# Assignment sums of two more heads folded on VectorE, a last store in two halves, and a re-searched instruction order, in a routing-attention and MLP kernel

## Chip, cores, metric

One core of one Trainium2 chip. The metric is the device time of one execution in microseconds (us). The fast runs of the kernel before lie between 290.9 and 292.1 us in all rounds, 0.4% apart; every comparison below is between kernels run in turns on the same chip. A ratio is the mean time of one kernel's fast runs over the mean of the other's fast runs of the same rounds, so it is not quite the ratio of the medians quoted beside it. Engine names in the profile: PE is TensorE (products), PEld its weight loads, DVE is VectorE, ACT is ScalarE, POOL is GpSimd, SP is SyncE, which issues transfers.

## The reference, cut to what matters

```python
# B, H, S, D = 4, 8, 768, 64: 32 heads in all; 16 centroids per head
q_assign = argmax(normalised(q) @ normalised(c).T)     # one cluster per query
k_assign = argmax(normalised(k) @ normalised(c).T)     # one cluster per key
mask   = q_assign[:, :, :, None] == k_assign[:, :, None, :]
scores = where(mask, q @ k.T / sqrt(D), -1e9)
x      = softmax(scores) @ v            # reshaped to 3072 tokens x 512
h      = x @ w_in                       # 512 -> 2048
out    = gelu_exact(h) @ w_out          # 2048 -> 512
```

## The kernel before: what the change touches

The kernel is a list of some 2,000 small operations, each with a name, an engine and its dependencies. One long string, the order table, gives the order in which they are emitted; each engine gets its own part of that order as its list of instructions. A word such as `lok2@DVE` also names the engine. So the table decides two things: what stands behind what on each engine, and which engine does an operation that several could do.

For each head `i` the cluster of every query and key is found so. A product with the centroids (kept as a high and a low half in fp16) gives the assignment sums; `amax` takes the maximum over the 16 clusters; `ge` compares with it and so writes one-hot rows; those are transposed by TensorE (early heads) or by a transfer (later heads) and written into `kqT`, where they act as the mask inside the score product. The sums come in two ways:

```python
    ACC = set(range(0, 8))
    ...
        def asn(w):
            ...
                if acc:      # two products of 16 columns, summed in PSUM
                    nc.tensor.matmul(o, t[:, js], c_cat[:, h, 0], start=True, stop=False)
                    nc.tensor.matmul(o, t[:, js], c_cat[:, h, 1], start=False, stop=True)
                else:        # one product of 32 columns
                    nc.tensor.matmul(o, t[:, js],
                                     c_cat[:, h].rearrange("p a c -> p (a c)"),
                                     start=True, stop=True)
        ...
        if not acc:
            def fold():      # VectorE adds the two halves: PSUM in, SBUF out
                nc.vector.tensor_reduce(
                    out=T["asb", i],
                    in_=T["asn", i].rearrange("p n w (a c) -> p n w c a", a=2),
                    axis=AX.X, op=ALU.add)
        def src():
            return T["asn", i] if acc else T["asb", i]
        def amax():
            nc.vector.tensor_reduce(out=T["amax", i], in_=src(), axis=AX.X, op=ALU.max)
        def ge():
            nc.vector.tensor_tensor(o[:, :, :, 0:C], src(),
                                    T["amax", i].to_broadcast([128, N, 2, C]),
                                    op=ALU.is_ge)
```

The second MLP layer is computed with fewer products by a scheme of sums and differences of its operands. Its 64 operand sums (S1 to S4) may run on VectorE, or on GpSimd where the table says `@POOL`:

```python
            o1 = add("DVE", 0.58, due, lambda eng, f=sums: f(eng, 1), gb,
                     take=[s_S], name=f"S1_{b}{n}", alt={"POOL": 1.85})
            o2 = add("DVE", 0.58, due, lambda eng, f=sums: f(eng, 2), [o1, *ga], name=f"S2_{b}{n}", alt={"POOL": 1.85})
            o3 = add("DVE", 0.58, due, lambda eng, f=sums: f(eng, 3), [o1, *ga], name=f"S3_{b}{n}", alt={"POOL": 1.85})
```

The softmax here doesn't subtract the row's maximum and nothing guards it: scores larger than these inputs give would overflow.

## Time and profile before

| | before |
|---|---|
| time, median of 3 runs (range) | 291.6 us (291.41 to 291.66) |
| span of the profiled run | 289.8 us |
| TensorE work (sum of median start-to-start distances) | 278.1 us |
| TensorE time lost in waits between first and last product | 6.9 us |
| busy: TensorE, VectorE, ScalarE, GpSimd | 98, 70, 81, 37% |

TensorE is the bound. It can gain only from fewer products or from fewer waits, and the waits add up to 6.9 us. The lines that show it stand in the prediction.

### The profile page before, as it was taken

How to read it: one execution, taken by the hardware profiler on the slowest of the kernel's cores; microseconds unless marked ns; L12 is line 12 of the kernel's file. 1: busy time of each engine (PE TensorE's matmuls, PEld its weight loads, DVE VectorE, ACT ScalarE, POOL GpSimd, SP SyncE). 2: the span in 40 equal slices, each digit the busy share in tenths (PEclk: the TensorE clock that was granted, in tenths of full speed). 3: DMA queues.
4: the chain of work that ended last, by engine and by line, in shares of the span. 5: the costliest groups of instructions: out<-in, count | busy, mean ns of one | idle time of the engine just before them, and what ended most of it. 6: DMA issues, size and time to landing. Idle time of an engine off the chain costs nothing.

```text
span 289.8 us, 8355 instructions
## 1 busy us (share of the span) xinstructions
PE 284.4 (98%) x3398; PEld 213.0 (73%) x3398; DVE 204.2 (70%) x494; ACT 235.1 (81%) x333; POOL 108.0 (37%) x148
## 2 busy tenths in 40 slices
PE   8999999999999999999999999999999999999995
PEld 6887766677677777765677878766687788756884
DVE  4989788397998778643489875725778833787863
ACT  4899988699799999977799988957699988599510
POOL 5898834609120631117202031605622271328000
PEclk9999999999999999999999999999999999999999
DMA  7999998899666799976479899753134213200023
GB/s 249 249 268 248 256 214 230 207 174 177 160 175 139 146 227 187 188 192 168 127 156 177 156 222 187 191 128 75 27 30 118 56 50 97 77 2 0 20 74 127
DMA packets 78038, 43.11 MB, mean 149 GB/s; under 512 B 55472, under 2 KB 78000, under 8 KB 78000
## 3 DMA queue, kind: packets, MB, share of 16 engines
q1 hardware_dynamic: 73488, 38.16, 57.7%
q0 software_dynamic: 4224, 4.19, 8.9%
q8 instruction: 26, 0.43, 0.6%
q10 hardware_dynamic: 288, 0.23, 0.3%
q14 instruction: 12, 0.10, 0.1%
HBM read 27.30 MB, written 6.29 MB: 116 GB/s over the span
## 4 chain that ended last, share of the span: by engine, by line
PE 96%; DVE 2%; ACT 1%; issue 0%; DVEq 0%
PE op L1233 25%; PE hp L918 22%; PE sc_ps L783 21%; PE x_ps L815 12%; PE fx_ps L1054 6%; PE asn_ps L615 2%; PE warm_ps L372 2%; PE tr_ps L573 2%; DVE kqT L714 1%; DVE kqT L723 1%; PE asn_ps L613 1%; PE asn_ps L612 1%; PE oh_ps L691 1%; ACT p_sb L792 1%; PE fin_ps L886 0%
## 5 line engine op out<-in xcount | busy, mean ns | idle before, releaser
L792 ACT ACTIVATE p_sb<-sc_ps 128x768 f16<-128x768 f32 x192 | 146.0, 810 | 9.7 <-PE sc_ps L783 6.8
L783 PE MATMUL sc_ps<-kqT 80*128 80x384 f16 x384 | 93.5, 325 | 0.6 <-DVE kqT L714 0.3
L918 PE MATMUL hp<-xt,w_in_sb 128*128 128x384 f16 x384 | 65.6, 326 | 0.0
L815 PEld LDWEIGHTS <-p_sb 128*128 128x128 f16 x1152 | 47.2, 97 | 10.4 <-DVE x_tok L842 0.6
L1233 PEld LDWEIGHTS <-g 128*128 128x128 f16 x480 | 45.3, 97 | 12.6 <-DVE g L948 0.2
L931 ACT ACTIVATE g<-hp 128x768 f16<-128x768 f32 x48 | 38.9, 810 | 19.0 <-PE hp L918 18.5
L918 PEld LDWEIGHTS <-w_in_sb 128*128 128x128 f16 x384 | 36.4, 98 | 22.9 <-issue 0.2
L815 PE MATMUL x_ps<-vaug,p_sb 128*128 128x65 f16 x1152 | 51.6, 193 | 0.0
L1233 PE MATMUL op<-w_out_sb,g 128*128 128x256 f16 x288 | 40.9, 272 | 0.0
L783 PEld LDWEIGHTS <-kqT 80*128 80x128 f16 x384 | 31.6, 98 | 4.7 <-DVE kqT L714 0.5
L1233 PE MATMUL op<-w_st,g 128*128 128x256 f16 x192 | 27.3, 272 | 0.0
L518 POOL TENSOR_TENSOR st<-k_raw,st 128x384 f16<-128x384 f32 x18 | 17.0, 943 | 24.9 <-DVE st L382 18.4
L518 POOL TENSOR_TENSOR st<-q_raw,st 128x384 f16<-128x384 f32 x21 | 19.8, 947 | 13.4 <-ACT st L380 8.6
L382 POOL CAST st<-q_raw 128x384 f16<-128x384 f32 x16 | 8.4, 531 | 40.9 <-DMA q_raw<-in_q_dram 24.9
L631 DVE TENSOR_REDUCE asb<-asn_ps 128x192 f32<-128x384 f32 x24 | 13.2, 551 | 14.8 <-PE asn_ps L615 14.6
L382 POOL CAST st<-k_raw 128x384 f16<-128x384 f32 x16 | 8.6, 537 | 35.4 <-DMA kqT<-st 16.3
L1233 PEld LDWEIGHTS <-S 128*128 128x128 f16 x192 | 18.0, 97 | 5.0
L842 DVE TENSOR_TENSOR x_tok<-x_ps,rec 128x384 f16<-128x384 f32 (+1 forms) x40 | 19.0, 476 | 1.1
L835 DVE RECIPROCAL rec<-x_ps 128x6 f32<-128x6 f32 (+1 forms) x40 | 7.4, 186 | 11.7 <-PE x_ps L815 10.7
L615 PEld LDWEIGHTS <-kqT 128*128 128x128 f16 x288 | 12.0, 96 | 3.4
L1233 PE MATMUL op<-w_st,S 128*128 128x256 f16 x96 | 13.9, 272 | 0.0
L1233 PE MATMUL op<-w_out_sb,S 128*128 128x256 f16 x96 | 13.8, 272 | 0.0
(125 smaller groups left out, 405.6 us busy)
## 6 DMA issues: line engine op xcount, KB each, us to landing
q_raw<-in_q_dram SPq DMA_DIRECT2D x32, 192.0 KB, 3.5
v_raw<-in_v_dram SPq DMA_DIRECT2D x32, 192.0 KB, 3.5
out_dram<-c SPq DMA_DIRECT2D x48, 128.0 KB, 2.0
k_raw<-in_k_dram SPq DMA_DIRECT2D x31, 192.0 KB, 3.4
w_in_sb<-in_moe_w_in_dram POOLq DMA_DIRECT2D x4, 512.0 KB, 10.4
w_out_sb<-in_moe_w_out_dram POOLq DMA_DIRECT2D x4, 512.0 KB, 8.6
kqT<-st SPq DMA_TRANSPOSE x22, 4.3
k_raw<-in_k_dram ACTq DMA_DIRECT2D x1, 192.0 KB, 3.2
```

The source lines that it names most:

```text
L382: engine[eng].tensor_copy(o, i)
L518: engine[eng].tensor_sub(t[:, :, D:2 * D], T[w + "raw", i], t[:, :, 0:D])
L615: nc.tensor.matmul(o, t[:, js], c_cat[:, h].rearrange("p a c -> p (a c)"), start=True, stop=True)
L631: nc.vector.tensor_reduce(out=T["asb", i], in_=T["asn", i].rearrange("p n w (a c) -> p n w c a", a=2), axis=AX.X, op=ALU.add)
L783: nc.tensor.matmul(s_ps[:, e, 0:QB], T["kT", i][0:D + C, c * 128:(c + 1) * 128], T["qT", i][0:D + C, t * QB:(t + 1) * QB], start=True, sto ...
L792: nc.scalar.activation(T["p", i, t][:, 2 * cp:2 * cp + 2, :], T["sc", i, t, cp][:, :, 0:QB], ACT_FN.Exp, bias=0.0, scale=float(scale))
L815: nc.tensor.matmul(o, T["p", i, t][:, ch, jj * 128:(jj + 1) * 128], vaugs[turn("va", i)][:, ch, 0:D + 1], start=(ch == 0), stop=(ch == N - 1))
L842: nc.vector.tensor_tensor(T["xtok", b][:, h // 2, j0:j0 + nn, h % 2 * D:(h % 2 + 1) * D], T["x", key][:, :, 0:D], T["rec", key].to_broadca ...
L918: nc.tensor.matmul(T["hp", hb, fp][:, e, 0:QB], w_in_sb[:, m, f * 128:(f + 1) * 128], T["xt", b][:, m, t * QB:(t + 1) * QB], start=(m == 0 ...
L931: nc.scalar.activation(T["g", hb][:, :, fp, :], T["hp", hb, fp][:, :, 0:QB], ACT_FN.Gelu, bias=0.0, scale=1.0)
L1054: nc.tensor.matmul(o, a[p](m), r[p](m), start=start and m == 0, stop=m == 1, skip_group_check=not start)
L1233: nc.tensor.matmul(T["op", b, key], a()[:, f, j * 128:(j + 1) * 128], w[:, f, :], start=(start and f == 0), stop=(f == NB - 1), skip_group ...
```

## The change

The intent: (1) heads 6 and 7 leave the two-product form, which takes products from TensorE and gives VectorE two folds; (2) the last product is made in two column halves, each added and stored by itself on a queue of its own, so that the end after the last product gets shorter; (3) the order was searched anew, with a refitted model of the durations.

```diff
-    ACC = set(range(0, 8))
+    ACC = set(range(0, 6))
@@ second MLP layer, the last product only
-                    for f in range(4 * n, 4 * n + 4):
-                        nc.tensor.matmul(T["op", b, key],
-                                         a()[:, f, j * 128:(j + 1) * 128], w[:, f, :],
+                    fs = range(NB) if last else range(4 * n, 4 * n + 4)
+                    cs = slice(128 * n, 128 * n + 128) if last else slice(0, DB)
+                    for f in fs:
+                        nc.tensor.matmul(T["op", b, key][:, cs],
+                                         a()[:, f, j * 128:(j + 1) * 128], w[:, f, cs],
@@ its addition and store, once per half n
+                if last:
+                    tail.append(add("DVE", 0.28, ... nc.vector.tensor_add(
+                        c21[:, 128 * n:128 * n + 128], p1[...], op[...]) ...
+                    ... add("SP", 0.36, ... dma_start(out=..., in_=c21[:, half]) ...,
+                        alt={"SP": 0.36, "ACT": 0.36})
@@ the order table: nearly every line differs. Around heads 6 and 7:
-  ... asnq7 loadv5 amax7 loadv7 sc2b1 av4a0 ge7 av4a2 sc5a0 exp2b1 asnk6 asnq6 amax6 ge6 sc5a2 ...
+  ... asnq6 sc3b0 exp3b1 av4a0 v6 exp3b0 loq9 fold6 sc5a0 av4a1 exp5a0 amax6 loadv14 ge7 av4a2 sc2b1 w4 loadv5 lok9 w5 exp2b1 ge6 ...
@@ and around two of the operand sums:
-  ... fc2_0_P5_0_1 S3_02 sc9a2 fc2_0_P6_0_1 ...        ... sc9b2 S3_03 rec8_1 ...
+  ... S2_03 S1_02 S3_02@POOL asnk14 S2_02 ...           ... fc2_0_P6_0_1 S3_03@POOL sc9a2 ...
```

The table has 27 filler products in front for 32, and 135 operations changed engine.

## The prediction

> **What bounds the kernel now.** I read the head of the page first, then the groups by shape, the windows, the chain of waits of the early stage, and the timeline of the last microseconds.
>
> ```profile
> span 289.8 us, 8355 instructions
> PE 284.4 (98%) x3398; PEld 213.0 (73%) x3398; DVE 204.2 (70%) x494; ACT 235.1 (81%) x333; POOL 108.0 (37%) x148
> ...
> PE 96%; DVE 2%; ACT 1%; issue 0%; DVEq 0%
> ```
>
> TensorE is busy for 284.4 of 289.8 us and carries 96% of the chain that ended last, at full clock in every slice. Busy time hides short waits, because a product of 128x32 is shown as 177 ns while the next one starts 25 ns later. So I took the distances between the starts of neighbouring products in the timeline, the median for each kind, and multiplied by the count: 278.1 us of work between the first filler product (1.36) and the last product's start, where 285.0 us passed. So about **6.9 us** of TensorE time is lost in small waits. Besides that come 1.36 us before the first product and some 3.5 us after the last. Nothing else can be won without taking products away.
>
> Where the 6.9 us lie: between the first scores (11.15) and the first product of the first MLP layer (44.76) the same count gives 31.2 us of work in 33.6 us, so **2.4 us** are lost there; the other 224 us up to 269 lose only about 4, in pieces of 0.05 to 0.16 us. The windows say why:
>
> ```profile
> 11.15:44.76 33.61, 32.77 (x574) 25.41 (x574) 28.70 (x76) 30.87 (x43) 26.30 (x39) 1.00 1.11 251
> 44.76:269.00 224.24, 224.24 (x2551) 164.07 (x2549) 156.88 (x373) 193.33 (x268) 74.83 (x85) 1.00 0.65 135
> 269.00:290.00 21.00, 17.61 (x161) 15.43 (x158) 11.86 (x28) 4.44 (x11) 0.00 (x0) 1.00 0.23 76
> ```
>
> The columns after the window's length are TensorE, weight loads, VectorE, ScalarE and GpSimd. In the early stage VectorE is busy 85% and ScalarE 92%; later VectorE is at 70%. And in the early stage the chain runs through VectorE, by the writes of the one-hot rows into kqT:
>
> ```profile
> 19.63 0.55 DVE kqT L714
> ...
> 20.21 0.55 DVE kqT L723
> 20.79 0.56 DVE kqT L714
> ...
> 21.39 0.57 DVE kqT L723
> ```
>
> Four of them end the wait for the scores at 22.00. Heads 6 and 7 are prepared in just this stage (the last assignment maximum of the unfolded kind starts at 33.5).
>
> [...]24 products with 16 columns start from 7.96 to 8.54, which is 0.58 / 23 = 25 ns each, and products with 32 columns are 25 ns apart too. [...]The trace has 1.7 to 2.0 us for nearly all 128 KB output stores[...].
>
> **Part 1: fold of heads 6 and 7.** The groups concerned:
>
> ```profile
> L631 DVE TENSOR_REDUCE asb<-asn_ps 128x192 f32<-128x384 f32 x24 | 13.2, 551 | 14.8 <-PE asn_ps L615 14.6
> L615 PE MATMUL asn_ps<-c_cat,kqT 128*128 128x32 f16 x288 | 12.9, 177 | 0.0
> L612 PE MATMUL asn_ps<-c_cat,kqT 128*128 128x16 f16 x96 | 5.8, 169 | 0.0
> L613 PE MATMUL asn_ps<-c_cat,kqT 128*128 128x16 f16 x96 | 5.8, 169 | 0.0
> ```
>
> Heads 0 to 7 use 2 x 12 products with 16 columns (96 + 96 over eight heads), later heads 12 with 32 columns (288 over 24 heads). For two heads 48 products become 24; each product costs 25 ns[...], so TensorE loses 24 x 25 = **0.60 us** of work, not the 24 x 169 ns that the busy column suggests. VectorE gains two folds of 0.551 us = **1.10 us**; the maximum and the comparison cost the same (0.348 against 0.358 us, and a median of 0.36 both ways). The fold lies between the assignment and the one-hot rows, so it lengthens the preparation of each of the two heads by some 0.3 to 0.5 us, in the stage where VectorE ends TensorE's waits. I take a quarter of the 1.10 us as given back: +0.3.
>
> **Part 2: the tail.** The lines:
>
> ```profile
> 285.57 1.04 PE L1233 MATMUL op<-w_st,g 128*128 128x256 f16 x8
> 285.77 0.42 DVE L1285 TENSOR_TENSOR c<-u,op 128x256 f32<-128x256 f32 x1
> 286.65 0.42 DVE L1279 TENSOR_TENSOR c<-p,op 128x256 f32<-128x256 f32 x1 [0.45 <-PE op L1233]
> ```
>
> The last product's addition takes 0.42 us, its store is issued at 287.10 and has landed at about 288.81 (1.71 us), and 1.0 us of closing semaphores follows. The change makes 16 products of 128 columns (16 x 56 ns = 0.90) out of 8 of 256 (8 x 109 = 0.87): +0.02. An addition of 128 columns I estimate at 0.29 us: this kernel's additions from PSUM take 0.356 us for 192 columns and 0.420 for 256, so 0.064 per 64.[...] But both halves lie in one bank, and in the new table the first half's addition stands behind the second half's products.[...] The second queue only helps where an issue of 0.33 us would be in the way; stores issue at 285.87, 286.30 and 287.10, so the last one waits for no queue now: 0.
>
> **Part 3: the new order.** It has 27 filler products for 32. The first 18 fillers run[...] (213 ns), later ones at 109 ns; in the new order 21 stand in front, and first the k transpose of head 0, then centroids, then q. Between the transposes and the first scores only 6 fillers are left where there were 14. Fillers bridge waits, so removing them saves only if the loads, casts and copies in front are early enough. Taken at face value the work in front of the first scores falls by 5 x 109 = 0.55 us; I take **-0.5**. The rest of the order moves the casts and copies of some 135 operations between ScalarE, VectorE and GpSimd, leaves TensorE's products in number as they are, and can only act on the lost 6.9 us. A search on a better model may take a tenth of that, **-0.6**; it may as well lose as much, as a model is an approximation and the waits it plays with are 0.1 us long.
>
> **Sum:** -0.6 (products) + 0.3 (folds) - 0.1 (tail) - 0.5 (start) - 0.6 (order) = -1.5 us; 291.6 - 1.5 = **290.1 us**.
>
> **Rivals.** (a) *VectorE takes it back.* The two folds and their latency stand fully on the early path: +1.1 instead of +0.3, and the new order finds no room: 291.5. For it: 85% busy, and the chain quoted above. Against it: the early stage's order was searched again with the folds in it. (b) *The order was the true brake.* If the small waits of the early stage fall from 2.4 to about 1 us and the later ones by a quarter, the gain is 0.6 + 0.5 + 1.4 + 1 = 3.5 us: 288.1. For it: the losses are real, and the model was refitted for it. Against it: TensorE is already never idle for long, and ScalarE at 92% leaves the early stage little freedom. (c) *The model is wrong somewhere and one long wait opens*, for example a transfer late for a head: each such wait costs 0.3 to 2 us, 291 to 293. For it: loads are moved about (DMA share 1.11 in the early stage, so full); against it: the order before, of the same kind, shows no wait above 0.5 us. (d) *The fewer fillers [...]only turn into waiting*: the start is worth 0, 290.6.
>
> **Range and chances.** All that could be won without fewer products is 6.9 us of waits, 0.6 + 0.5 of work and a few tenths of tail; 2% is 5.8 us, so it would need nearly all of the waits to vanish: 3%. Slower by 2% needs several waits of kind (c): 2%. The range adds about 1.7 us either way, between rivals (b) and (a): 288.4 to 291.8.
>
> **What would show each step.** Products: L612 and L613 72 each, L615 312, sum of TensorE's work by medians about 277 us. Folds: L631 x26, and the early stage's lost time at 2.4 us or below. Tail: two additions of about 0.29 us; the first beginning before the last product ends, or after it, tells the two cases apart; end of the last product to end of span stays 3.1 to 3.3 us. Start: first scores at about 10.6. Order: total lost time about 6.3 us. I am wrong if the lost time moves by more than 2 us either way, or a wait of TensorE over 1 us appears.

## The result, and the profile after

| | before | after |
|---|---|---|
| time, median of 4 runs (range) | 291.5 us (291.07 to 291.66) | 295.24 us (294.83 to 296.89) |
| ratio, 95% interval | | 1.0141 (1.0101 to 1.0181) |
| span of the profiled run | 289.8 | 295.1 |
| TensorE work | 278.1 | 276.7 |
| TensorE time lost | 6.9 | 13.6 |
| VectorE time over the medians | 10.3 (19 instructions) | 19.2 (28 instructions) |

The kernel became 1.4% slower: within 2%, as most of the chances had it, but 5 us from the predicted time and far outside the range. The last row is made so: in each group of VectorE instructions of one kind and shape, those that lasted over 0.25 us longer than the group's median, and the sum of what they lasted longer. I call them stretched. (Grouped by program line as well, the sums are 10.3 and 17.5 us.)

The head of the page of the kernel after, its clock line and its chain:

```profile
span 295.1 us, 8322 instructions
PE 285.2 (97%) x3377; PEld 212.5 (72%) x3377; DVE 207.5 (70%) x487; ACT 236.3 (80%) x331; POOL 125.2 (42%) x160
...
PEclk9999989999999999999999999999999999999999
...
PE 89%; DVE 6%; ACT 2%; DMA 1%; issue 1%; POOL 0%; ACTq 0%; DVEq 0%
```

GpSimd went from 108.0 to 125.2 us of work, and VectorE's share of the chain from 2 to 6%. The groups show the first as ten more operand sums: GpSimd ran 9 of the shape 128x768 before and 19 after, at 1.64 to 1.70 us each, so 10 x 1.67 = 16.7 of the 17.2 us. One slice, the sixth, had a lower clock. The windows (length; TensorE, weight loads, VectorE, ScalarE, GpSimd busy; clock; DMA share; GB/s):

```profile
11.15:44.76 33.61, 30.78 (x508) 23.45 (x506) 28.33 (x68) 28.80 (x41) 25.45 (x39) 0.95 1.13 252
44.76:269.00 224.24, 221.86 (x2554) 162.94 (x2553) 156.54 (x364) 191.83 (x259) 85.54 (x92) 1.00 0.65 135
```

In the early stage TensorE is busy 2 us less in the same stretch, and later, where it had been busy for all of 224.24 us, it now stands for 2.4 us while GpSimd does 10.7 us more.

What TensorE waited for, before and then after (line waited for, us in total, times, longest; left out are the 1.4 us before the first filler, in both, a wait of 0.2 us before and one of 0.5 us for ScalarE after):

```profile
PE sc_ps L783 <- DVE kqT L714: 0.3, 1, 0.3
PE tr_ps L573 <- DVE kqT L714: 0.2, 1, 0.2
```

```profile
PE oh_ps L691 <- DVE oh L652: 2.2, 1, 2.2
...
PE op L1239 <- DVE g L948: 1.0, 1, 1.0
PE sc_ps L783 <- DVE kqT L714: 0.8, 2, 0.6
PE tr_ps L573 <- POOL st L518: 0.5, 1, 0.5
```

Three of these four wait for VectorE, on instructions that cost 0.35 to 0.6 us when undisturbed. Were they late, or long? The comparison `ge` (L652) by tile: count, duration in ns as least/median/most, first and last start. First the kernel before, then after:

```profile
L652 DVE TENSOR_TENSOR oh<-asb,amax x24: 316/358/1301, 49.3 to 221.3; 128x192 f16<-128x192 f32 x24
...
L652 DVE TENSOR_TENSOR oh<-asn_ps,amax x6: 345/357/358, 15.3 to 33.9; 128x192 f16<-128x192 f32 x6
```

```profile
L652 DVE TENSOR_TENSOR oh<-asb,amax x26: 343/357/1717, 32.4 to 231.6; 128x192 f16<-128x192 f32 x26
L652 DVE TENSOR_TENSOR oh<-asn_ps,amax x4: 348/358/359, 14.6 to 24.5; 128x192 f16<-128x192 f32 x4
```

They were long. The comparison that reads PSUM never lasts over 0.36 us; the same comparison with both inputs in SBUF has the same median and a longest of 1.72 us. The kernel before showed this already, in the heads that it folds: a longest of 1.30 us, and a mean of 537 ns at a median of 358. And the timeline of the kernel after shows beside what (start, duration, engine, line, operation):

```profile
32.04 0.51 POOL L382 CAST vaug<-v_raw 128x384 f16<-128x384 f32 x1
...
32.37 2.96 DVE L652 TENSOR_TENSOR oh<-asb,amax 128x192 f16<-128x192 f32 x2
32.52 0.90 POOL L518 TENSOR_TENSOR st<-q_raw,st 128x384 f16<-128x384 f32 x1
33.38 0.78 POOL L467 DMA_DIRECT2D w_out_sb<-in_moe_w_out_dram  x1
...
34.18 0.92 POOL L518 TENSOR_TENSOR st<-k_raw,st 128x384 f16<-128x384 f32 x1
...
35.38 0.51 PE L691 MATMUL oh_ps<-ident,oh 128*128 128x128 f16 x6 [2.17 <-DVE oh L652]
```

Two comparisons, of heads 7 and 6, take 1.72 and 1.32 us instead of 0.36 each, while GpSimd has one instruction after the other. The transposes of the one-hot rows wait for both, and after that wait TensorE runs at a granted clock of 0.50 from 36.20 to 39.61 us: neighbouring transposes start 106 ns apart in that time, and 56 ns apart in the rest. That is the dent in the clock line.

The same picture, later, with an operand sum on GpSimd:

```profile
85.01 3.60 POOL L948 TENSOR_TENSOR g<-g 128x768 f16<-128x768 f16 x2 [4.35 <-DMA k_raw<-in_k_dram]
...
87.40 1.43 DVE L714 TENSOR_SCALAR kqT<-ohT 16x768 f16<-16x768 f16 x1
...
88.88 0.50 PE L783 MATMUL sc_ps<-kqT 80*128 80x384 f16 x2 [0.57 <-DVE kqT L714]
89.45 0.35 DVE L714 TENSOR_SCALAR kqT<-ohT 16x768 f16<-16x768 f16 x1
```

The write of one-hot rows takes 0.35 us undisturbed (last line), but 1.43 us where the second of two GpSimd sums (up to 88.61) runs beside it. It ended at 88.83, 0.22 us after GpSimd. The scores wait for it.

These are not single cases. Counted over all 18 traces (before, after and e1 to e16), in groups of one operation, tiles and shape: 405 VectorE instructions lasted over 0.25 us longer than their median, and every one of them ran beside GpSimd for about as long as it was lengthened. All their operands lay in SBUF. Of the 4703 VectorE instructions with an operand in PSUM none lasted even 0.02 us longer than its median.

Last, the groups that answer to those of part 1, and the tail:

```profile
L631 DVE TENSOR_REDUCE asb<-asn_ps 128x192 f32<-128x384 f32 x26 | 14.4, 553 | 16.0 <-PE asn_ps L615 15.8
L615 PE MATMUL asn_ps<-c_cat,kqT 128*128 128x32 f16 x312 | 14.0, 177 | 0.0
L612 PE MATMUL asn_ps<-c_cat,kqT 128*128 128x16 f16 x72 | 4.5, 170 | 0.0
```

```profile
290.84 1.06 PE L1239 MATMUL op<-w_st,g 128*128 128x128 f16 x16
...
291.94 0.48 DVE L1255 TENSOR_TENSOR c<-p,op 128x128 f32<-128x128 f32 x2 [0.43 <-PE op L1239]
```

The counts of products and folds are as predicted, and both half additions start after the sixteenth product.

### The profile page after: what moved, and what is told of

Its sections match the earlier page's. It is cut to its first block, busy times and chain, and to the rows that moved or that the text cites.

```text
span 295.1 us, 8322 instructions
## 1 busy us (share of the span) xinstructions
PE 285.2 (97%) x3377; PEld 212.5 (72%) x3377; DVE 207.5 (70%) x487; ACT 236.3 (80%) x331; POOL 125.2 (42%) x160
## 4 chain that ended last, share of the span: by engine, by line
PE 89%; DVE 6%; ACT 2%; DMA 1%; issue 1%; POOL 0%; ACTq 0%; DVEq 0%
PE op L1239 24%; PE hp L918 21%; PE sc_ps L783 20%; PE x_ps L815 11%; PE fx_ps L1054 6%; PE asn_ps L615 2%; PE tr_ps L573 2%; ACT p_sb L792 1%; DVE kqT L714 1%; DMA k_raw<-in_k_dram 1%; DVE oh L652 1%; DVE g L948 1%; PE oh_ps L691 1%; PE fin_ps L886 1%; DVE wf L972 1%; PE asn_ps L612 1%
## 5 line engine op out<-in xcount | busy, mean ns | idle before, releaser
L792 ACT ACTIVATE p_sb<-sc_ps 128x768 f16<-128x768 f32 x192 | 146.4, 810 | 13.9 <-PE sc_ps L783 10.8
L1239 PE MATMUL op<-w_out_sb,g 128*128 128x256 f16 x288 | 40.1, 272 | 1.0 <-DVE g L948 1.0
L1239 PE MATMUL op<-w_st,g 128*128 128x256 f16 (+1 forms) x200 | 27.4, 268 | 0.0
L518 POOL TENSOR_TENSOR st<-k_raw,st 128x384 f16<-128x384 f32 x22 | 20.6, 940 | 14.1 <-DVE st L382 13.1
L631 DVE TENSOR_REDUCE asb<-asn_ps 128x192 f32<-128x384 f32 x26 | 14.4, 553 | 16.0 <-PE asn_ps L615 15.8
L518 POOL TENSOR_TENSOR st<-q_raw,st 128x384 f16<-128x384 f32 x22 | 20.6, 934 | 7.6 <-DVE st L382 4.9
L382 POOL CAST st<-q_raw 128x384 f16<-128x384 f32 x18 | 9.7, 537 | 32.7 <-DMA k_raw<-in_k_dram 13.3
L1239 PEld LDWEIGHTS <-S 128*128 128x128 f16 x192 | 17.9, 97 | 4.1
L382 POOL CAST st<-k_raw 128x384 f16<-128x384 f32 x15 | 7.9, 527 | 21.6 <-DMA kqT<-st 13.6
L948 POOL TENSOR_TENSOR g<-g 128x768 f16<-128x768 f16 x8 | 13.5, 1696 | 7.3 <-DMA k_raw<-in_k_dram 4.4
L1316 POOL TENSOR_TENSOR c<-u,p 128x256 f32<-128x256 f32 x4 | 3.3, 832 | 30.0 <-DMA out_dram<-c 30.0
L835 DVE RECIPROCAL rec<-x_ps 128x6 f32<-128x6 f32 (+1 forms) x40 | 7.5, 187 | 11.3 <-PE x_ps L815 10.5
L382 POOL CAST vaug<-v_raw 128x384 f16<-128x384 f32 x18 | 9.5, 533 | 13.8 <-DMA v_raw<-in_v_dram 7.7
```

The lines of the kernel that those rows point to most:

```text
L382: engine[eng].tensor_copy(o, i)
L518: engine[eng].tensor_sub(t[:, :, D:2 * D], T[w + "raw", i], t[:, :, 0:D])
L631: nc.vector.tensor_reduce(out=T["asb", i], in_=T["asn", i].rearrange("p n w (a c) -> p n w c a", a=2), axis=AX.X, op=ALU.add)
L792: nc.scalar.activation(T["p", i, t][:, 2 * cp:2 * cp + 2, :], T["sc", i, t, cp][:, :, 0:QB], ACT_FN.Exp, bias=0.0, scale=float(scale))
L948: engine[eng].tensor_sub(o, a, c)
L1239: nc.tensor.matmul(T["op", b, key][:, cs], a()[:, f, j * 128:(j + 1) * 128], w[:, f, cs], start=(start and f == 0), stop=(f == NB - 1), sk ...
```

## The experiments

**Theory P (theory A in the expectations).** VectorE instructions whose operands lie in SBUF are held up while GpSimd works, as in the 405 cases above; the new order gives GpSimd more and longer instructions and puts them beside VectorE's urgent ones. **Rivals:** F, the fold's own length on the path to the one-hot rows; L, loads or transfers that come late in the new order; T, the tail; D, that any change of engines inside a tuned order costs, whatever the engine. The kernels' results in one table; "GpSimd" is its busy time, "stretched" VectorE's time over the medians, "lost" TensorE's lost time, all in us and from the profiled run.

| run | change in short | time (range) | ratio to before (95%) | GpSimd | stretched | lost |
|---|---|---|---|---|---|---|
| before | | 291.5 | 1 | 108.0 | 10.3 | 6.9 |
| after | | 295.24 (294.83–296.89) | 1.0141 (1.0101–1.0181) | 125.2 | 19.2 | 13.6 |
| e1 | after, no fold | 294.53 (294.03–294.96) | 1.0103 (1.0088–1.0119) | 126.2 | 16.6 | 10.3 |
| e2 | after, four words moved | 295.08 (293.61–296.09) | 1.0119 (1.0086–1.0153) | 125.9 | 16.0 | 10.3 |
| e3 | after, 5 sums to VectorE | 293.18 (292.50–293.72) | 1.0050 (1.0032–1.0067) | 116.8 | 12.4 | 10.5 |
| e4 | after, engines of before | 320.36 (318.02–321.37) | 1.0979 (1.0932–1.1025) | 108.7 | 14.5 | 35.5 |
| e5 | before + fold | 292.70 (291.87–292.95) | 1.0038 (1.0025–1.0051) | 108.9 | 12.2 | 7.8 |
| e6 | before + tail | 291.46 (291.31–291.90) | 1.0004 (0.9992–1.0016) | 108.3 | 11.3 | 7.5 |
| e7 | before, 4 sums to GpSimd | 297.03 (296.56–300.00) | 1.0226 (1.0188–1.0264) | 115.2 | 14.2 | 11.6 |
| e8 | before + start of after | 291.99 (291.82–292.68) | 1.0023 (1.0011–1.0035) | 107.8 | 11.4 | 8.9 |
| e9 | e5, maxima in PSUM | 292.58 (291.78–293.06) | 1.0032 (1.0014–1.0050) | 108.6 | 13.0 | 8.2 |
| e10 | e2 and e3 | 295.59 (295.06–296.22) | 1.0142 (1.0123–1.0161) | 117.0 | 13.8 | 11.8 |
| e11 | after, again | 294.45 (293.91–299.11; without 299.11, a slow run, 293.98) | 1.0096 (1.0076–1.0115) | 125.4 | 17.9 | 10.7 |
| e12 | after, all three repairs | 291.61 (291.15–293.29) | 1.0013 (0.9991–1.0034) | 117.2 | 11.4 | 8.0 |
| e13 | e12 without the earlier split | 292.87 (291.91–294.22) | 1.0038 (1.0016–1.0060) | 117.5 | 10.4 | 10.8 |
| e14 | after, maxima in PSUM only | 295.08 (293.78–298.07) | 1.0128 (1.0092–1.0165) | 125.6 | 15.8 | 10.9 |
| e15 | after, earlier split only | 295.29 (293.22–296.12) | 1.0114 (1.0090–1.0138) | 125.4 | 19.9 | 12.0 |
| e16 | e12, two more moves | 293.24 (291.67–294.96) | 1.0049 (1.0021–1.0076) | 117.1 | 10.3 | 8.4 |

e1 to e4 shared one chip, as did e5 to e8, e9 to e12 and e13 to e16; before took 291.4 to 291.7 us on each. All results were correct.

**e1: the fold undone in the new order.**

```diff
-    ACC = set(range(0, 6))
+    ACC = set(range(0, 8))
-  ... fold7 ... fold6 ...           (and ge7 directly behind amax7)
```

> The changed kernel with heads 6 and 7 unfolded again (24 more products, no folds; the comparison of head 7 stands before head 6's products, since both need the one PSUM bank). Everything else, GpSimd's order too, as in the changed kernel. Theory A[...]: in the changed kernel the two comparisons of heads 6 and 7 took 1.72 and 1.32 us instead of 0.36, because they now read two tiles in SBUF (folded sums and maxima) and stood behind GpSimd's instructions; unfolded they read one tile in PSUM and one in SBUF, so they take 0.36 us, TensorE's wait of 2.2 us before the one-hot transposes of heads 6 and 7 shrinks to under 0.5 us, and the time falls by 1.5 to 2 us against the changed kernel's 295.2: about 293.4. Theory B (the fold's own length and the new order of VectorE make the wait): the comparisons stay long or the wait stays over 1 us; the time stays at 294.5 to 295.5. The rest, against 291.5 of before, is the later waits that this run leaves in place.

The two comparisons, with sums in PSUM again, took 0.357 and 0.358 us beside the same GpSimd work, so the stretch at 33 us is due to the operand's place. The one-hot transposes began at 34.59 instead of 35.38. But the time fell by only 0.6 us against e2 of the same chip, where 1.5 to 2 us had been expected, and the intervals overlap. The undoing brings a cost of its own: head 6's assignment products wait 0.58 us for head 7's comparison, as both heads need one bank. So e1 shows why the comparisons were long, not what the fold costs.

**e2: four operations moved out of the comparisons' way.**

```diff
-  ... ge7 av4a2 sc2b1 w4 loadv5 lok9 w5 ... ge6 ... putk7 loadq8 sc5a2 putq7 ...     (loq9 before fold6)
+  ... ge7 av4a2 sc2b1 loadv5 ... ge6 ... putk7 loadq8 sc5a2 putq7 loq9 w4 lok9 w5 ...
```

> The changed kernel, folds kept; only four instructions that GpSimd executes (two splits of head 9, two weight loads) moved behind the one-hot writes of heads 6 and 7, so GpSimd has nothing to do in SBUF while the two comparisons run. Theory A[...]: both comparisons take 0.36 us, the wait of 2.2 us falls under 0.5 us, time about 293.2. Theory B (the fold itself is too long): the wait stays, 295.

My premise was wrong. GpSimd's own list has no words between the old and the new places, so no engine's list changed: e2 is the program of after. It has one use: with after and e11 it gives three sets of runs of one program, 295.24, 295.08 and 294.45 us (293.98 without its slow run), single fast runs from 293.6 to 296.9 (before: 290.9 to 292.1). In its profile the two comparisons took 0.63 and 0.65 us, not 1.72 and 1.32: how the instructions meet at 33 us changes from run to run.

**e3: five operand sums back to VectorE.**

```diff
-  S3_02@POOL S3_03@POOL S4_03@POOL S3_22@POOL S2_21@POOL
+  S3_02 S3_03 S4_03 S3_22 S2_21
```

> The changed kernel with five sums of the second MLP layer (batch 0: third sum of blocks 2 and 3 and fourth sum of block 3; batch 2: second sum of block 1 and third sum of block 2) back from GpSimd to VectorE, where the kernel before has them. Theory A[...]: TensorE's waits of 0.73, 0.38 and 1.13 us between 88 and 95 us and of 0.70 us at 224 us, each behind a VectorE instruction that stood behind a GpSimd sum of 1.65 us, mostly vanish; VectorE gets 5 x 0.58 us more work, beside TensorE; time 295.2 - 2 to 2.5 = 292.9. Theory C (the waits there come from VectorE being overfull in the new order): more work on VectorE makes them longer, time 295.5 or more.

1.9 us faster than e2 on the same chip, with intervals apart (1.0032 to 1.0067, against 1.0086 to 1.0153). VectorE got 5 x 0.58 = 2.9 us more work and was busy for less, 203.0 us for 204.4 in e2's profile and 207.5 in after's. That speaks for P. The lost time in the one profile, 10.5 us, does not show the gain; a profile is one run, e3's of its slowest (293.72) and e2's of its fastest (293.61).

**e4: the new order with the old engines.** Every operation that both tables hold got the engine of before.

> The changed kernel's order, folds and tail, with the engine of each instruction that both kernels have as in the kernel before (some 130 instructions move back; GpSimd's work falls from 125 us towards 108). Theory A (the loss is the new assignment to GpSimd[...]): lost TensorE time falls from 13.6 us to 8 to 10, time 292 to 293. Theory D (the order, not the assignment, is at fault): time stays near 295 or rises, since order and assignment were searched together.

320 us: the order was made for its engines. The chain of waits of e4 holds transposing transfers of 5 to 6 us that nothing hid:

```profile
90.56 5.79 DMA kqT<-st
```

The run says nothing between P and F; it says that an order and its assignment are one thing (theory D, for a change of everything at once).

**e5: the fold alone, in the order of before.**

```diff
-    ACC = set(range(0, 8))
+    ACC = set(range(0, 6))
-  ... amax7 ...   ... amax6 ...
+  ... fold7 amax7 ...   ... fold6 amax6 ...
```

> The kernel before with nothing but the fold of heads 6 and 7 (two folds of 0.55 us on VectorE, 24 products fewer), its own order otherwise. By the count TensorE has 0.6 us less work. Theory A[...]: the comparisons of heads 6 and 7 now read two tiles in SBUF and can stand behind GpSimd, which is busy about 78% of the time there: each is lengthened by 0 to 1 us, and the wait before the one-hot transposes of heads 6 and 7 grows by 0.5 to 1.5 us: time 291.2 to 292.5.[...]

+1.1 us by the ratio, as much as both folds in full, and 0.6 us of products saved on top are gone too; the median lies above the 291.2 to 292.5 expected. **e9** asks whether P explains it: the maxima of heads 6 and 7 are written into the unused columns of the bank that held the sums, so that the comparison has one input in PSUM and one in SBUF.

```diff
 e9, against e5 (heads 6 and 7)
-            T["asn", i] = pool["m"].tile([128, N, 2, W], FP32, ...)
+            bank = pool["m"].tile([128, 512], FP32, ...)      # sums in columns 0:384
-            T["amax", i] = pool["amax"].tile(...)
+            T["amax", i] = bank[:, 480:492]                   # bank set free by ge, not by fold
```

> The kernel before with the fold of heads 6 and 7 as in e5, but their maxima written into unused columns of the same PSUM bank instead of SBUF, so that the comparison again reads only one tile from SBUF (the folded sums). Work on VectorE and TensorE as in e5. Theory A[...]: the two comparisons take 0.36 us instead of 0.67 and 0.55, whatever GpSimd does; the time falls from e5's 292.7 to 291.0 to 291.6. Rival E (what costs in e5 is the two folds themselves, 1.1 us more on VectorE and a longer way to the one-hot rows): it stays at 292.3 to 292.8 though the comparisons are short.

The timelines of e5, then of e9:

```profile
32.16 0.67 DVE L647 TENSOR_TENSOR oh<-asb,amax 128x192 f16<-128x192 f32 x1
```

```profile
32.14 0.35 DVE L657 TENSOR_TENSOR oh<-asb,asn_ps 128x192 f16<-128x192 f32 x1
...
32.55 0.46 PE L618 MATMUL asn_ps<-c_cat,kqT 128*128 128x32 f16 x12 [0.29 <-DVE oh L657]
```

The comparison is short again, 0.35 for 0.67 us, and the time is the same: 292.58 for 292.70. The transposes of the one-hot rows stand at 34.32 us in e5 and 34.45 in e9, with 0.74 and 0.75 us lost before them. I took this for the fold's length (F) and against P, but e9 does not decide it. Since its maxima lie in the bank of the sums, head 6's assignment products now wait for head 7's comparison (the last line above): 0.45 us of lost time that e5 does not have, and about what the two comparisons save (0.31 and 0.19 us). How the cost of e5 divides between the fold's length and P stays open.

**e6: the tail alone, in the order of before.**

```diff
-  ... c122_3 stc1223 c212_3 stc2123
+  ... c122_3 ... c212_3x c212_3y stc2223@ACT stc1223@ACT stc2123x@ACT stc2123y
```

> The kernel before with nothing but the tail of the change (column halves on two queues, and the last stores of the other corners on the second queue). In the changed kernel both half additions began after the last product, and from their start to the end of the span 3.16 us passed, against 3.15 us in the kernel before: I expect the same time within 0.1 us.[...]

Ratio 1.0004: the tail is worth nothing, as predicted within 0.1 us. Theory T falls.

**e7: the converse of e3.** Four of those sums go to GpSimd in the order of before, nothing else.

```diff
-  S3_02 S3_03 S4_03 S2_21
+  S3_02@POOL S3_03@POOL S4_03@POOL S2_21@POOL
```

> The kernel before with four sums of the second MLP layer (batch 0: third sum of blocks 2 and 3, fourth sum of block 3; batch 2: second sum of block 1) on GpSimd instead of VectorE, as in the changed kernel. VectorE is relieved of 4 x 0.58 us. Theory A[...]: VectorE's instructions beside them stand until GpSimd's sum of 1.65 us is over; total lengthening of VectorE rises by 2 to 4 us and the time by 0.5 to 2.5 us, to 292 to 294. [...]the sums themselves take 1.65 instead of 0.58 us and could be waited for directly: the trace tells the two apart.

+5.6 us by the medians, more than the whole change and far over the 292 to 294 expected; one of the four runs, 300.00 us, had a clock of 0.987. The timeline of e7:

```profile
84.21 1.80 POOL L943 TENSOR_TENSOR g<-g 128x768 f16<-128x768 f16 x1 [0.96 <-DVE S L1148]
84.55 1.88 DVE L943 TENSOR_TENSOR S<-S,g 128x768 f16<-128x768 f16 x1
...
86.48 0.39 PE L1228 MATMUL op<-w_st,S 128*128 128x256 f16 x2 [1.35 <-DVE S L943]
...
87.01 1.76 DVE L943 TENSOR_TENSOR w_st<-w_out_sb,w_st 128x512 f16<-128x512 f16 x1
```

A sum of 0.58 us on VectorE takes 1.88 us, from 0.34 us after GpSimd's start to 0.41 us after its end, and TensorE stands 1.35 us for it; two more such waits lie within 5 us. These are not waits for the moved sums themselves: what TensorE waits for is VectorE's. That is P with the cause put in by hand.

**e8: the start alone.** The words of after up to the first scores, then those of before.

> The kernel before with the changed kernel's order up to the first scores (27 fillers instead of 32; one load left at its old place). In the changed kernel the first scores began at 10.55 us instead of 11.15. If that gain lasts, 0.6 us faster: 290.9; if the early stage, with ScalarE busy 92% of it, takes it back, the same: 291.5.

The first scores come at 10.19 us for 11.15, and the kernel is 0.6 to 0.7 us slower: TensorE then loses 0.49, 1.18 and 0.61 us between 16 and 24 us, behind a load of q that took 8.4 us to land and the splits after it. The first MLP product comes at 45.86 for 44.60. What was won at the start is given back within 15 us (L).

**e10, e11: e2 and e3 joined, and after once more.** As e2 changes nothing, e10 is the program of e3.

> The changed kernel with both moves of e2 and e3 (GpSimd quiet beside the comparisons of heads 6 and 7; five sums of the second MLP layer back on VectorE). If the two causes add: 295.2 - 2.0 (e3) - 0.2 to 2 (e2) = 291.2 to 293.0; no wait of TensorE over 1 us but the one at 19.6 us (0.7 to 1.2 us, a load that comes late). If other stretched instructions take their place: 293 or more.

> The changed kernel itself once more, on this chip and with a second profile. I expect 295.2 +- 0.7 and, in the profile, the same long waits in the same places (at 19.6, 33, 88, 95 and 224 us, together 4.5 to 6 us)[...].

On this chip the order turned round: e10 at 295.59, after at 293.98 in its fast runs. In e10 the comparisons at 33 us took 1.81 and 1.23 us, the wait in its profile was 2.18 us (2.17 in after's), and the clock was 0.987 to 0.994 in all four runs; in e3's profile that wait had been 1.34 us. e11's profile did not repeat after's long waits, as had been expected: there was none at 20 us, and 0.63 us at 33. So one program lies at 293.2 or at 295.6 by how instructions meet at 33 us, and e3 alone does not prove the price of the sums. The meeting had to be taken away first.

**e12: three repairs together.** The five sums of e3; the maxima in PSUM of e9 (`ge7` directly behind `amax7`, and the assignment products of head 6 behind `sc3b0`); and the split of head 4 ahead of the cast of head 6 on GpSimd, as TensorE waits for that split at 19.6 us while the cast stands in front of it and waits for a load.

```diff
-  ... hik6 ... lok4 ...
+  ... lok4 ... hik6 ...
```

> The changed kernel with all found causes taken away at once: the five sums on VectorE; the maxima of heads 6 and 7 in PSUM as in e9 (for that the comparison of head 7 stands before head 6's products and these one place later); the split of head 4 before the cast of head 6 on GpSimd, which waits for a late load. If the explanation is whole, all waits over 0.7 us are gone, the lost TensorE time is about 8 us as in the kernel before, and the time is 290.5 to 291.5, at or just under the kernel before. If it is not whole, 292 or more, and the trace shows what is left.

291.61 us, the time of before. The head of its page, and its two comparisons:

```profile
PE 282.7 (98%) x3377; PEld 210.8 (73%) x3377; DVE 202.6 (70%) x492; ACT 236.0 (82%) x331; POOL 117.2 (40%) x155
```

```profile
L657 DVE TENSOR_TENSOR oh<-asb,asn_ps x2: 353/353/353, 31.0 to 32.9; 128x192 f16<-128x192 f32 x2
```

Stretched time is 11.4 us for 19.2, and lost time 8.0 for 13.6. The time lies a hair outside the range named, one loss over 0.7 us is left in the profile (0.77 at 6.0 us), and the profiled run was the second fastest of six, up to 293.29 us.

**e13, e14, e15: which of the three.** e13 is e12 without the earlier split; e14 has the maxima in PSUM alone; e15 the earlier split alone.

> As e12, but the split of head 4 stays behind the cast of head 6 on GpSimd. [...]291.6 to 292.4, with the wait at 19.6 us (0.7 to 1.2 us) present in some runs and no wait over 0.7 us at 33, 88, 95 us. If the late split is what drags the rest: 293 or more.

> The changed kernel with only the maxima of heads 6 and 7 in PSUM (and the order of heads 7 and 6 that this needs). GpSimd has all its sums. [...]comparisons of 0.36 us, wait at 33 us under 0.8 us, waits at 88 to 95 and 224 us as in the changed kernel; time 293.5 to 294.3, so 1 to 1.7 us under the changed kernel, and no run with a clock under 0.998.

> The changed kernel with only the split of head 4 before the cast of head 6 on GpSimd. The wait at 19.6 us goes. Alone: 0.3 to 1 us under the changed kernel, 294.2 to 294.8; if the late split is also what brings GpSimd beside the two comparisons of heads 6 and 7, more: 293.5, with a wait at 33 us of 0.6 to 0.8 us in the profile.

e14 against e13 is the clean pair: one chip, the comparisons at 33 us short in both, and only the five sums differ. 295.08 and 292.87 us, ratios 1.0128 and 1.0038, intervals apart: **the sums on GpSimd cost about 2.2 us.** Two of e14's six runs (298.07 and 296.22) had a clock of 0.994, against the expectation that none would; the profile is of another run, so what happened in them is not known. Without them e14's median is 294.46 and the cost 1.6 us. Theory D does not explain this pair: the order had been searched with these sums on GpSimd, and moving them off it made it faster. The maxima in PSUM alone gain nothing that can be told from after's spread, nor does the earlier split alone (295.08 and 295.29 us, where 293.5 to 294.3 and 294.2 to 294.8 were expected; after itself was not run on this chip). e12's ratio is 0.25% under e13's, but the intervals overlap and the chips differ. e13 still has an occasional wait late in the kernel, in its profile 1.3 us, for a transposing transfer:

```profile
186.99 5.92 DMA kqT<-st
```

e15 shows the same. The new order leaves these transfers little room.

**e16: e12 and two more moves** (the assignment products of head 6 ahead, and one result copy from ScalarE to VectorE).

> e12 with two more moves: the assignment of head 6 one more product group later (its wait of 0.64 us for head 7's comparison), and one copy of the second MLP layer of batch 2 from ScalarE to VectorE (ScalarE waited 0.6 us for it, and TensorE then 0.6 us for ScalarE). If both waits go and nothing takes their place: 290.7; I expect 290.7 to 291.6, at most 0.3% under the kernel before.

293.24 us, where 290.7 to 291.6 was expected: the wait moved to 30.5 us (0.90) and to 219.6 us (0.95). No version beat the kernel before; e12 ties with it.

## Why the prediction was wrong

**Products: right.** L612 and L613 came to 72 each and L615 to 312, VectorE's folds to 26; TensorE's work fell by 278.1 - 276.7 = 1.4 us, where 0.6 and 0.55 had been worked out, and "about 277" was named as the sign. The rest is the measure: it prices five fillers at 213 ns, 1.06 us.

**Tail: right.** The additions took 0.29 and 0.28 us and both began at 291.94 us or later, after the last product: the second of the two cases named among the signs; that the shared bank is the reason is not shown. From the start of the first to the end of the span 3.16 us passed, 3.15 before. The -0.1 us in the sum was my estimate. Whether half the bytes shorten the last store is not settled: the last 64 KB store took 1.70 us from issue to landing in the kernel after and 1.57 in e6, the last 128 KB store 1.69 before.

**Start: near at the first scores, with luck, and wrong beyond.** They came at 10.55 (10.6 was named). But two more profiles of the same program have 10.96 and 10.97, and four variants with the start of before have 10.75 to 11.12 where before has 11.15, so about 0.4 us of either is chance. And e8 shows that the gain did not last: rival (d), and a bit worse.

**Fold: mis-sized.** "I take a quarter of the 1.10 us as given back: +0.3". Alone in the order of before it cost 1.1 us net (e5), or 1.7 with the 0.6 of saved products counted. Rival (a) had named +1.1, by length alone; whether the length or P made it is open (e9).

**The failed step: "can only act on the lost 6.9 us", and "the maximum and the comparison cost the same".** The step treats an instruction's duration as its own, and an assignment as neutral as long as the engine has time to spare. Taken so, the order moved at most a tenth of 6.9 us, and more work for GpSimd cost nothing: the step speaks of casts and copies and does not mention the ten sums. Neither holds. The median of the comparison did stay 0.357 us; in heads 6 and 7 it went from at most 0.358 to 1.72 and 1.32 us, for both of its inputs now lay in SBUF. The "median of 0.36 both ways" hid this: the groups read for the prediction had a mean of 537 ns for the form with two inputs in SBUF. And VectorE's stretched time rose by 19.2 - 10.3 = 8.9 us in all, 2.3 us of it in these two comparisons. That part of this reached TensorE is what e7 and e14/e13 show: about 2.2 us by five sums in the new order (1.6 without e14's two runs at a lower clock), 5.6 us by four in the old one. Lost time, for which 6.3 us was predicted, was 10.3 to 13.6 in three profiles of the same program; that it would not move by over 2 us, and that no wait over 1 us would appear, were the prediction's own signs. Rival (c) had the form, waits of 0.3 to 2 us, with 291 to 293; but it looked for a late transfer, and there are several waits, mostly of another kind.

**Two readings that do not hold.** "1.7 to 2.0 us for nearly all 128 KB output stores" is true of 28 of the 48; a quarter took over 2.5 us. And in the stage from 11.15 to 44.76 us the same count by medians gives 30.2 us of work, so 3.2 us are lost there, not 2.4. Neither changes the argument.

What the runs show of it: the comparison with one input in PSUM took 0.36 us at most in all 18 traces, with two in SBUF up to 1.81 us (e10); the `tensor_scalar` that writes kqT from SBUF took 1.43 us for 0.35; of 1034 instructions of `tensor_reduce` (the folds and the maxima) none was stretched, the longest fold 0.56 us. The trace of before had the two forms of the comparison side by side, 0.36 us at most against up to 1.30 us. I drew on that neither for the fold, which turns a comparison of the first form into one of the second, nor for the sums. Why GpSimd's work lengthens the one form and not the other, no run shows.

**What adds up, and what stays open.** Work -1.4 us and lost time +6.7 us give the +5.3 us between the two profiled spans. Of the median's +3.7 us, the five sums are shown to be about 2.2 (1.6 by the narrower count). With sums, maxima and split repaired (e12), lost time is still 8.0 - 6.9 = 1.1 us above before, which takes up most of the work saved: the kernel ties. How this last part divides among the fold (e5, e9), the start (e8) and the transfers that come close (e13, e15) is not settled; the single effects do not add, and the meeting at 33 us falls out differently from run to run.

## What to carry to other kernels

Before work is given to an engine with time to spare, ask what will run beside it, and look in a trace at what instructions last there: here 1.65 us of GpSimd stood in place of 0.58 us of VectorE, and with five such sums taken back (e3) VectorE was busy for 203.0 us where it had been busy for 204.4 and 207.5 (e2, after). When a change moves an operand from PSUM to SBUF, look at the instructions that read it later, and at their mean and longest durations rather than their medians (here 537 ns and 1.30 us at a median of 358 ns); where the kernel already runs the new form elsewhere, as here, its trace has the answer before the change is made. And where a profile shows one long wait, run the same program again before pricing it: here one program gave 293.2 and 295.6 us.

## What the traces showed besides

- Where GpSimd's instructions stand back to back, the order of the starts did not tell which one ends first. In the kernel after, the comparison started at 32.37 us, in the last 0.2 us of a GpSimd cast; the split that GpSimd began at 32.52 ended at 33.42, and the comparison at 34.09. It was lengthened by 1.36 us, while the longest of the GpSimd instructions beside it lasted 0.90 us. In e2, the same program, a comparison that started at 32.10 us inside a cast took 0.63 us.
- Whether GpSimd's work for a DMA lengthens a comparison as well, no run here separates. The first long comparison at 33 us ended 0.66 us after the split beside it in after and 0.75 in e10, both times while GpSimd worked at a DMA issue or 0.02 us after; one with a split alone beside it ended 0.21 us after it (e5: 32.83 against 32.62). But in e11 a comparison ended 0.22 us after the split with such an issue under way (33.53 against 33.31).
- In the kernel after, the clock fell after a single wait of 2.17 us: for 3.41 us products ran at half speed (granted clock 0.50, 106 ns for 56). In e10 the same followed a wait of 2.18 us, and the clock was 0.987 to 0.994 in all four runs; waits of 1.35 and 1.44 us (e7, a clock of 1.000 in the profiled run) were not followed by it.
